# Spectral mixing and a feed-forward layer: a new start-up for the first batch, and a row operation that reads PSUM

## The chip, the cores and the metric

One core of one Trainium2 chip. The metric is the device time of one execution in microseconds (us). The kernel before took 1954.14 us (median of 3 runs, 1953.02 to 1954.99) when the prediction was made.

In what follows PE is the matmul engine, DVE the vector engine, ACT the scalar engine, POOL the general engine, and SP the engine that only issues DMAs. PSUM is the memory that PE writes to, cut into banks. "Half clock" means that the record of PE's granted clock shows 0.5.

## The reference

```python
batch, seq, dim = 8, 3008, 256
X = fft(fft(x, axis=1), axis=2).real           # Fourier mixing over sequence and features
h = X.reshape(24064, 256) @ w_in               # 256 -> 2048
g = h * (1 / (1 + exp(-1.702 * h)))            # quick GELU
out = g @ w_out                                # 2048 -> 256
```

## The kernel before

The sequence transform is done in two stages (3008 = 47 x 64). For each batch the rows of `x` are folded (even and odd parts), multiplied by cosine and sine tables, spilled to DRAM and read back in another order, rotated, and multiplied again ("stage 2"). Then 48 steps per batch form the hidden layer and the output: 384 steps in all, software-pipelined. "Nyquist's product" is a small extra product of one row, for the highest frequency; "warm-up" matmuls are products that nobody reads, there to keep PE busy and its clock up. A step makes two hidden products P and Q in two PSUM banks (`pa`, `pb`), builds two mirrored rows from their sum and difference, applies GELU, and feeds output products three steps later.

The parts that matter here are the start-up of the first batch and the rows of a step.

```python
def fold_first(r, m):                  # first batch, one of eight pieces
    ...
    nc.scalar.copy(dst(e[:], 0, H, 2), src(xt[:], 0, H, 2))                      # a tiny copy, on ACT
    nc.vector.tensor_tensor(dst(e[:], 1, 1, H - 1), ..., op=ALU.add)             # 128 partitions
    for p, eng in ((slice(0, 64), nc.vector), (slice(64, 128), nc.gpsimd)):      # DVE and POOL side by side
        eng.tensor_tensor(dst(e[p], H + 1, 1, H - 1), ..., op=ALU.subtract)

def mix_first(r, m):
    ...                                # matmuls of the piece into one bank
    nc.scalar.copy(xt[:, q:q + 2, :]..., ps[:])        # also ACT, in order with the tiny copy

def rows(t):
    ...
    nc.vector.tensor_tensor(two(h[:], n), two(v[:], n), two(pb[:], n), op=ALU.add)   # v: ACT's copy of pa
    ...                                # dif = nb * af2 - pb, twice
    ins = [... for x in (v, dif)]      # last row operation: two operands from SBUF
    nc.vector.tensor_tensor(free(h[:], 512 + at + m - 1, ...), *ins, op=ALU.add)

# start-up (cut)
for p in idle:                         # partitions of x's tile that hold no data are zeroed
    for eng, z in ((nc.vector, slice(0, 16)), (nc.gpsimd, slice(16, 32))):
        eng.memset(xt[p, z, :], 0.0)
load_in(0, nc.sync)                    # first weight chunk, ahead of x
nc.scalar.dma_start(out=w1[:], in_=tab1)
load_first(0, 4, nc.sync); load_first(4, 4, nc.scalar); load_first(8, 8, nc.sync)
...
for r in range(2):
    for m in range(4):
        fold_first(r, m)
        mix_first(r, m)
    spill(0, 8 * r, 8 * r + 8, (nc.sync, nc.scalar))
```

The weights arrive as 64-bit floats and are rounded on the core in eight chunks: three operations on ACT (`bounds`), three on DVE, and a clamp and an addition on POOL. In the kernel before, the first three chunks are given to `bounds` with `nc.gpsimd`: two of ACT's three operations are then on POOL. Rounding is spread over the start-up and the first steps.

## Time and profile before

| what | where it is read | before |
|---|---|---|
| PE busy over the whole run | busy shares | 98% |
| first hidden product starts | timeline | 63.91 us |
| seventh hidden product starts, PE dense from here | timeline | 104.54 us |
| PE busy from 148 to 1940 us | windows | 1792.00 of 1792.00 us |

The windows view of the kernel before shows how the start-up looked. Its columns are the stretch, its length, busy us of PE, of PE's weight load, of DVE, ACT and POOL, each with its count, then the granted clock, the DMA share and GB/s.

```profile
20.00:30.00 10.00, 4.61 (x18) 2.09 (x18) 10.00 (x8) 1.05 (x3) 9.55 (x6) 0.50 1.06 256
30.00:40.00 10.00, 5.94 (x26) 2.61 (x26) 10.00 (x10) 2.50 (x8) 7.66 (x6) 0.50 0.44 137
40.00:50.00 10.00, 8.08 (x28) 3.57 (x29) 0.92 (x1) 1.97 (x5) 3.47 (x2) 0.53 0.11 19
```

PE sits at half clock for almost all of it (last column but two). From 20 to 40 us DVE is busy all the time, and POOL nearly so; from 40 to 50 us they have finished their folds and PE still works through pieces that wait for each other on ACT.

### The profile page before, as it was taken

The numbers are of one execution on the slowest core, as the hardware profiler recorded it, in microseconds if no ns is written. First come the engines' busy times: TensorE is split into PE (matmuls) and PEld (weight loads), VectorE is DVE, ScalarE is ACT, GpSimd is POOL, SyncE is SP. The second block draws the span as 40 slices with busy tenths as digits, with TensorE's granted clock in tenths as the row PEclk, the third lists the DMA queues.
The fourth block names the chain that finished last, engine by engine and source line by source line (L and its number), as shares of the span: only waits on it lengthen the run. The fifth ranks groups of instructions, "written<-read, shape, count | busy, mean of one in ns | idle before, by whom it ended". The sixth has DMA issues, their size and how long they took to land.

```text
span 1952.1 us, 29356 instructions
## 1 busy us (share of the span) xinstructions
PE 1916.0 (98%) x10664; PEld 1672.3 (86%) x10664; DVE 1586.4 (81%) x2925; ACT 665.0 (34%) x921; POOL 816.1 (42%) x1057
## 2 busy tenths in 40 slices
PE   6899999999999999999999999999999999999998
PEld 2588888988889888898888888898888988889887
DVE  6688788888888887897788877888887888778876
ACT  1533333333333333333333333333333333333332
POOL 6476322652236432463225622265223643223222
PEclk6899999999999999999999999999999999999999
DMA  6732442227212282033621254322632224202201
GB/s 170 225 62 28 82 77 26 48 43 110 27 15 47 47 119 17 12 55 50 108 17 20 49 98 58 28 46 45 95 40 16 18 43 60 17 12 23 20 12 22
DMA packets 242311, 102.78 MB, mean 53 GB/s; under 512 B 207749, under 2 KB 232069, under 8 KB 238905
## 3 DMA queue, kind: packets, MB, share of 16 engines
q1 hardware_dynamic: 239154, 98.22, 32.5%
q10 hardware_dynamic: 3011, 2.69, 0.5%
q8 instruction: 83, 1.36, 0.3%
q14 instruction: 63, 0.51, 0.1%
HBM read 57.60 MB, written 47.67 MB: 54 GB/s over the span
## 4 chain that ended last, share of the span: by engine, by line
PE 96%; ACT 1%; DVE 0%; DVEq 0%; issue 0%
PE po L496 58%; PE pa L429 17%; PE pb L429 17%; PE ps L207 1%; PE ps L304 1%; PE psw L398 0%; PE ps L211 0%; PE psa L404 0%; ACT wcs L399 0%; ACT r L354 0%; ACT r L353 0%; ACT g L346 0%; PE psn L321 0%; ACT h L458 0%; ACT L458 0%; PE psr L291 0%
## 5 line engine op out<-in xcount | busy, mean ns | idle before, releaser
L470 POOL TENSOR_TENSOR s<-h 128x256 f32<-128x256 f32 (+1 forms) x376 | 269.5, 717 | 1060.5 <-ACT h L458 996.3
L496 PE MATMUL po<-s,wt 128*128 128x256 f32 (+1 forms) x2256 | 599.7, 375 | 0.0
L433 ACT COPY v<-pa 128x512 f32<-128x512 f32 (+1 forms) x384 | 221.8, 577 | 1065.0 <-PE pa L429 1064.9
L496 PEld LDWEIGHTS po<-s,wt 128*128 128x128 f32 x2256 | 428.6, 190 | 48.3
L443 DVE TENSOR_TENSOR h<-v,pb 128x512 f32<-128x512 f32 (+1 forms) x384 | 258.7, 674 | 260.0 <-PE pb L429 252.5
L496 PE MATMUL po<-h,wo 128*128 128x256 f32 (+1 forms) x1632 | 469.6, 375 | 0.0
L453 DVE TENSOR_TENSOR h<-v,dif 128x512 f32<-128x512 f32 (+1 forms) x448 | 413.4, 934 | 13.2
L458 ACT ACTIVATE h<-h 128x1024 f32<-128x1024 f32 (+1 forms) x384 | 400.7, 1043 | 19.6 <-DVE h L453 19.5
L429 PE MATMUL pa<-pq,wcs 128*128 128x256 f32 (+1 forms) x1536 | 395.8, 380 | 0.0
L429 PE MATMUL pb<-pq,wcs 128*128 128x256 f32 (+1 forms) x1536 | 388.8, 376 | 0.0
L496 PEld LDWEIGHTS po<-h,wo 128*128 128x128 f32 x1632 | 310.1, 190 | 35.5
L429 PEld LDWEIGHTS pa<-pq,wcs 128*128 128x128 f32 x1536 | 287.8, 191 | 47.8 <-issue 14.5
L446 DVE SCALAR_TENSOR_TENSOR dif<-nb,af,pb 128x256 f32<-128x256 f32 (+1 forms) x768 | 328.0, 468 | 0.5 <-DMA nb<-pq 0.5
L429 PEld LDWEIGHTS pb<-pq,wcs 128*128 128x128 f32 x1536 | 292.9, 191 | 33.6
L471 POOL TENSOR_TENSOR s<-h 128x256 f32<-128x256 f32 (+1 forms) x376 | 287.0, 763 | 0.0
L474 DVE TENSOR_TENSOR s<-h,s 128x256 f32<-128x256 f32 (+1 forms) x376 | 216.8, 576 | 13.0
L496 PE MATMUL po<-s,wo 128*128 128x256 f32 (+1 forms) x752 | 220.4, 375 | 0.0
L496 PE MATMUL po<-h,wt 128*128 128x256 f32 (+1 forms) x752 | 220.4, 375 | 0.0
L473 DVE TENSOR_TENSOR s<-s,h 128x256 f32<-128x256 f32 (+1 forms) x376 | 182.1, 484 | 4.7 <-POOL s L470 4.7
L496 PEld LDWEIGHTS po<-s,wo 128*128 128x128 f32 x752 | 142.9, 190 | 16.1
L496 PEld LDWEIGHTS po<-h,wt 128*128 128x128 f32 x752 | 142.9, 190 | 16.1
L193 POOL TENSOR_TENSOR xt<-xt 128x510 f32<-128x510 f32 x56 | 75.9, 1355 | 4.4
(66 smaller groups left out, 755.5 us busy)
## 6 DMA issues: line engine op xcount, KB each, us to landing
out_dram<-os SPq DMA_DIRECT2D x568, 32.0 KB
Td<-xt SPq DMA_DIRECT2D x14, 768.0 KB
t<-Td SPq DMA_DIRECT2D x7, 1536.0 KB
xt<-in_x_dram SPq DMA_DIRECT2D x15, 512.0 KB
nb<-pq SPq DMA_DIRECT2D x23, 256.0 KB
out_dram<-os SPq DMA_DIRECT2D x192, 28.0 KB
Xr<-in_x_dram SPq DMA_DIRECT2D x7, 752.0 KB
Xr<-in_x_dram SPq DMA_DIRECT2D x7, 705.0 KB
```

Of the source, the lines that this page charges most:

```text
L193: eng.tensor_tensor(low, low, free(t, up + D - 1, [-D, 2], [-1, D - 1]), op=ALU.add)
L429: nc.tensor.matmul(ps[:, i * 256:i * 256 + n], lhsT=wcs[cs][:, f * 128:(f + 1) * 128], rhs=pq[:, cs, ks], start=True, stop=True)
L433: nc.scalar.copy(two(v[:], n), two(pa[:], n))
L443: nc.vector.tensor_tensor(two(h[:], n), two(v[:], n), two(pb[:], n), op=ALU.add)
L446: nc.vector.scalar_tensor_tensor(dif[:, i * 256:i * 256 + n], nb[:, ks], af2[:, f:f + 1], pb[:, i * 256:i * 256 + n], op0=ALU.mult, op1=AL ...
L453: nc.vector.tensor_tensor(free(h[:], 512 + at + m - 1, [256, 2], [RUN, blocks], [-1, m]), *ins, op=ALU.add)
L458: nc.scalar.activation(g, g, ACTF.Gelu_apprx_sigmoid)
L470: eng.tensor_tensor(s1, a21, a22, op=ALU.add)
L471: eng.tensor_tensor(s3, a11, a21, op=ALU.subtract)
L473: eng.tensor_tensor(s2, s1, a11, op=ALU.subtract)
L474: eng.tensor_tensor(s4, a12, s2, op=ALU.subtract)
L496: nc.tensor.matmul(pot[q][:, i, :n], lhsT=lhs, rhs=rhs, start=(p == 0 and i == 0 and f == 0), stop=(p == NP - 1), skip_group_check=True)
```

## The change

Its intent is a shorter start-up. The first batch sits on 94 neighbouring partitions (2 x 47), so no partition of its tile has to be zeroed before loading and the fold needs no POOL; `x` is loaded ahead of the first weight chunk; each fold runs one piece ahead of its products; Nyquist's product moves behind the first hidden product; one weight chunk is rounded per step. `bounds` no longer gets `nc.gpsimd`, so two operations of each of the first three chunks move from POOL to ACT. Apart from that, the last row operation reads P's bank and not ACT's copy of it.

```diff
-    for p in idle:
-        for eng, z in ((nc.vector, slice(0, 16)), (nc.gpsimd, slice(16, 32))):
-            eng.memset(xt[p, z, :], 0.0)
-    load_in(0, nc.sync)
-    nc.scalar.dma_start(out=w1[:], in_=tab1)
+    nc.scalar.dma_start(out=w0, in_=tab1[:, 0:n0 + 1])
     load_first(0, 4, nc.sync)
     load_first(4, 4, nc.scalar)
     load_first(8, 8, nc.sync)
-    nc.sync.dma_start(out=small[:], in_=tab2)
+    nc.scalar.dma_start(out=small[:], in_=tab2)
+    load_in(0, nc.scalar)
...
+    fold_first(0)
+    for k in range(8):
+        if k < 7:
+            fold_first(k + 1)
+        else:
+            bounds(("in", 0))
+        mix_first(k)
+        if k % 4 == 3:
+            spill(0, 2 * k - 6, 2 * k + 2, (nc.sync, nc.scalar if k == 7 else nc.sync))
...
-                ins = [... for x in (v, dif)]
+                ins = [... for x in (pa, dif)]
...
         if t < n:
             hidden(t)
+        if t == 0:
+            nyquist_weights(0)
+            nyquist(0, 0)
```

Cut here: the tables (the first batch's sign is now folded into a second copy of the table, made by one DVE operation), the fold on 94 partitions with two DVE operations, the order of the rounding, loading the later batches' table during step 3, and the warm-up matmuls (`warm(10)` in place of `warm(12)` at the start, and a new `warm(4)` behind the last piece).

## The prediction

> **What bounds the kernel now.** I read the page's busy shares first, then the windows view (busy time of each engine by stretch), then the timeline of the first 110 us.
>
> ```profile
> PE 1916.0 (98%) x10664; PEld 1672.3 (86%) x10664; DVE 1586.4 (81%) x2925; ACT 665.0 (34%) x921; POOL 816.1 (42%) x1057
> ...
> 64.00:100.00 36.00, 33.99 (x132) 25.78 (x133) 28.90 (x34) 27.24 (x33) 15.22 (x9) 0.92 0.77 203
> 100.00:148.00 48.00, 47.32 (x298) 41.64 (x297) 38.44 (x64) 16.95 (x26) 33.86 (x40) 1.00 0.32 66
> 148.00:1940.00 1792.00, 1792.00 (x10046) 1584.05 (x10045) 1479.12 (x2789) 609.84 (x840) 727.81 (x984) 1.00 0.31 44
> 1940.00:1952.00 12.00, 3.88 (x18) 3.06 (x17) 3.89 (x9) 0.37 (x1) 0.00 (x0) 0.80 0.29 44
> ```
>
> In the last four lines the columns are the stretch, its length, then busy us of PE, PE's weight load, DVE, ACT and POOL, the clock, the DMA share and GB/s. From 148 to 1940 us PE is busy in 1792.00 of 1792.00 us at full clock. That matmul work is untouched by the change, so there is nothing to win there: only a new wait could lose something. Whatever is won lies before about 104 us, and shows as an earlier start of the dense part. So I follow the chain of the head.
>
> ```profile
> 14.48 1.28 ACT L346 ACT_TABLE_LOAD   x1 [14.48 <-DMA xt<-in_x_dram]
> 17.93 0.21 ACT L246 COPY e<-xt 128x8 f32<-128x8 f32 x1 [1.03 <-DMA xt<-in_x_dram]
> 39.20 0.58 ACT L262 COPY xt<-ps 128x512 f32<-128x512 f32 x1 [2.24 <-PE ps L259]
> 39.68 0.21 ACT L246 COPY e<-xt 128x8 f32<-128x8 f32 x1
> 39.99 1.98 PE L259 MATMUL ps<-e,w 128*64 128x256 f32 x8 [0.96 <-issue]
> 42.13 0.58 ACT L262 COPY xt<-ps 128x512 f32<-128x512 f32 x1 [2.24 <-PE ps L259]
> 48.62 0.37 ACTq L279 DMA_DIRECT2D Td<-xt  x1
> 53.60 0.38 SPq L285 DMA_DIRECT2D t<-Td  x1
> 57.81 0.56 PE L291 MATMUL psr<-t,small 128*128 128x4 f32 x2 [3.79 <-DMA t<-Td]
> 63.91 2.08 PE L429 MATMUL pa<-pq,wcs 128*128 128x256 f32 x4
> 83.52 0.69 DVE L453 TENSOR_TENSOR h<-v,dif 128x512 f32<-128x512 f32 x1
> 88.82 2.67 DVE L453 TENSOR_TENSOR h<-v,dif 128x512 f32<-128x512 f32 x1
> 104.54 1.13 PE L429 MATMUL pa<-pq,wcs 128*128 128x256 f32 x4
> ```
>
> These timeline lines give start, length, engine, operation and the idle time before. The first batch's folds start at 17.93, because the input arrives after a weight chunk, the tables and two memsets of its own tile. A piece then takes 2.93 us (39.20 to 42.13): matmuls 1.98 at half clock, their copy 0.58, then the tiny fold copy 0.21, on the same in-order engine behind it. The spill to DRAM is issued at 48.62; its result is back for the rotation at 57.81, the first hidden product is at 63.91, and the seventh, from which PE has no wait, at 104.54.
>
> **What the Trainium skill says.** "TensorE: Matmul & The Clock Gate", Part 1 on the clock gate: after an idle window of about 3.4 us PE falls to half clock, and needs about as long busy to come back. The trace agrees: the windows view has 1.00 from 0 to 10 us, 0.94 and 0.50 in the next two tens, with 7.1 us idle before the first fold product. "GPSIMD Engine Reference", Key points: it shares SBUF interfaces with VectorE and collides with instructions that have two SBUF inputs. It agrees: the fold sum takes 0.67 us, or 1.57 beside a busy POOL; the last row operation 0.69 or up to 2.67 (above). "DMA: Bandwidth & Descriptors", Queues, rings and completion order: each DMA engine takes packets in turn from the queues that have work. The DMA view of before agrees as far as it shows both queues moving at once (0.57 and 0.31 MB in the first five us).
>
> **The change, part by part.**
>
> *x first, and the memsets.* DMA is saturated from 2 to about 32 us. By bytes: in 10 to 25 us, mostly x, 0.89 + 0.95 + 0.81 MB took 15 us, so x runs at about 0.175 MB per us; wide rows (weight chunks, 25 to 30 us) reach 0.35 to 0.4. Before the last x piece lands the change still moves x (3.0 MB, 17.1 us), the table (0.82 MB, 2.1 us), and probably the small table and the first weight chunk (1.4 MB, 3.7 us), which sit on the other queue and take turns. With 1.9 us to start: about 25 us for the last piece, against some 26.5 before. The first piece lands at about 11 us instead of 17.9.
>
> *Folds ahead of products.* On 94 partitions POOL has no fold work left, so each fold is two DVE operations of 0.67 instead of up to 1.57 twice. Pieces 0 to 3 run in about 13 to 18 us. Then PE waits for x until about 25 (7 us idle), falls to half clock, and pieces 4 to 7 start at 25 + 1.4 = 26.5. The tiny copy is now ahead, so the pitch is PE's own 2.0 us instead of 2.93: the last ends at about 34.6. Here I see a price: ACT's three operations for the first weight chunk (1.12 + 1.06 + 1.06, about 3.3 us, the lengths of the trace) stand before the last copy out of PSUM. That copy starts about 36.5 and ends at 37.1, against 48.59 before.
>
> *Spill and return.* 48.6 to 57.8 is 9.2 us, mostly DMA round trips; the first half is spilled early but the return needs both. I keep 9.2: rotation at 46.3.
>
> *Rotation to hidden product.* Before 6.1 us. Nyquist (2.0 us) moves behind the first hidden product, and stage 2 (1.96 at half clock, 1.1 at full) may be faster: I take 3.5. First hidden product at about 49.8 instead of 63.9: minus 14.
>
> *The ramp.* Before it took 104.5 - 63.9 = 40.6 us to hidden product 7. Now it carries more: Nyquist and the first weight row (about 1.9 us on PE), and the rounding of out chunk 0. Per step DVE has about 2.3 us of rows and 1.23 + 0.69 + 1.23 of rounding, 5.4; ACT 3.3 of bounds, 0.58 + 1.06, and every second step 1.2 of weight copies, 4.9 to 6.1. PE itself has 1.7 hidden, 3.45 product from step 3, and 5.1 of weight folding every second step. All three are close, so little is absorbed. P's bank is now freed by the last row operation, not by ACT's copy; with four banks in turn, the weight row of the same step wants it. Measured in the trace of before, the end of that operation lies up to 3.9 us after the reuse of the bank in steps 0 to 5. Against that the operation reads PSUM, has one SBUF input and should cost 0.69 instead of 1.7 to 2.7 there. I take 42.5 us for the ramp: dense at 92.3, minus 12.
>
> *The steady part.* The last row operation drops from a mean of 1.06 to about 0.69 us, 320 x 0.37 = 120 us of DVE time. It is worth nothing: DVE isn't the bound. The bank is held longer; in the trace of before the smallest gap between the end of the last row operation and the reuse of P's bank is 0.57 us once the ramp is over (usually 4.7), except one step of the first batch (-1.0). Shorter operations widen that. I expect no wait.
>
> Sum: 1954.1 - 12 = 1942.
>
> **The rivals.** (1) x isn't overtaken by the small table and weight chunk, lands at 21 to 22, PE stays warm and the pieces finish four to six us sooner: 1936. For it: it is what the order is meant for; against it: turn-taking, and these two are issued at about 11 us, when half of x is outstanding. (2) The held bank makes PE wait in the ramp behind DVE, whose rounding is interleaved; each step loses one to two us: 1947 to 1950. For it: the negative gaps above; against it: the cheaper row operation. (3) The held bank stalls the dense part: even 0.3 us in each of 384 steps would be 115 us and 2060. Against it are the gaps of 0.57 and more, so I give it one in a hundred. (4) A large gain from freeing 120 us of DVE: excluded by PE's 1792.00.
>
> **Range and chances.** The terms that can move are x's arrival (+-3 us), the ACT detour (0 to 3) and the ramp (+-4). Together about +-7: 1935 to 1949. Faster by over 2% needs 39 us, more than the head has to give when dense must still start after 25 us of x and a 9 us round trip: 0.01.
>
> **What would show it.** Right: first fold copy at about 13, a PE gap of some 7 us ending near 26, clock 0.5 after it; the spill's second half issued near 37; rotation near 46; first hidden product near 50; PE's busy time equal to the stretch from about 95 on; last row operation near 0.69 us. Wrong: any PE wait on a DVE row operation after 150 us, a spill before 33 (rival 1), or a dense start after 97 (rival 2).

## The result

The changed kernel took 1941.72 us (median of 4 runs, 1941.08 to 1943.03), the kernel before 1954.07 us beside it (4 runs). The ratio is 0.9938, with a 95% interval from 0.9921 to 0.9955. A ratio here is the mean time of one kernel's runs over that of the other's of the same rounds, so it is not quite the ratio of the quoted medians. The predicted time was 1942.0.

The busy shares of the changed kernel:

```profile
PE 1908.7 (98%) x10730; PEld 1673.0 (86%) x10730; DVE 1409.5 (73%) x2924; ACT 671.6 (35%) x927; POOL 756.3 (39%) x1045
```

DVE has 1409.5 us of work in place of 1586.4, and PE is at 98% as it was. The windows view of the changed kernel, with columns as above:

```profile
20.00:30.00 10.00, 2.09 (x26) 1.88 (x24) 2.91 (x5) 1.20 (x4) 1.09 (x1) 0.80 1.07 244
30.00:40.00 10.00, 7.95 (x62) 5.51 (x58) 5.10 (x7) 7.38 (x11) 1.38 (x1) 0.86 0.49 160
40.00:50.00 10.00, 5.51 (x76) 2.93 (x77) 1.54 (x5) 5.18 (x8) 2.07 (x2) 0.99 0.71 237
...
136.00:1927.00 1791.00, 1791.00 (x10041) 1583.04 (x10040) 1323.47 (x2788) 609.94 (x839) 698.94 (x984) 1.00 0.31 44
```

The last line is the steady part: PE is again busy in every microsecond, 1791.00 of 1791.00. From 20 to 30 us, by contrast, nobody but the DMA has much to do (DMA share 1.07): everybody waits for `x`. The timeline of the changed kernel's start-up gives the chain:

```profile
13.85 5.01 DVE L251 TENSOR_TENSOR e<-xt 94x508 f32<-94x508 f32 x8 [5.89 <-DMA xt<-in_x_dram]
27.07 0.21 ACT L249 COPY e<-xt 94x8 f32<-94x8 f32 x1 [6.66 <-DMA xt<-in_x_dram]
28.52 5.80 PE L261 MATMUL ps<-e,wt 128*64 128x127 f32 x64 [7.91 <-DVE e L251]
34.01 1.14 ACT L346 ACTIVATE g<-raw 128x1024 f32<-128x1024 f32 x1
37.21 0.57 ACT L263 COPY xt<-ps 128x512 f32<-128x512 f32 x1
37.80 0.36 ACTq L279 DMA_DIRECT2D Td<-xt  x1
46.98 0.36 PE L291 MATMUL psr<-t,small 128*128 128x4 f32 x2 [2.24 <-DMA t<-Td]
49.63 1.85 PE L429 MATMUL pa<-pq,wcs 128*128 128x256 f32 x4 [1.21 <-DVE pq L310]
92.38 1.13 PE L429 MATMUL pa<-pq,wcs 128*128 128x256 f32 x4
```

Folds start at 13.85. `x`'s last piece lets ACT and DVE go on at 27.07, and PE's gap of 7.91 us ends at 28.52. Pieces 4 to 7 take 5.80 us of PE. Their last copy, however, starts at 37.21, because ACT does the first weight chunk from 34.01 on. The spill is issued at 37.80, the rotation starts at 46.98, the first hidden product at 49.63 and the seventh at 92.38. So the first hidden product comes 14.3 us earlier than before, and the seventh 12.2 us.

The waits of PE in the changed kernel up to 1940 us (what waited, for whom, us in total, times, longest) all lie in the start-up and the first steps. Lines shorter than 2 us are left out, except for one:

```profile
PE ps L261 <- DVE e L251: 7.9, 1, 7.9
PE psw L398 <- POOL wst L368: 3.1, 1, 3.1
PE ps L261 <- issue: 2.9, 1, 2.9
PE psr L291 <- DMA t<-Td: 2.2, 1, 2.2
PE psa L404 <- ACT wcs L399: 2.1, 3, 0.8
...
PE psw L398 <- DVE h L453: 1.4, 1, 1.4
```

The last one is where the held bank shows: PE's fold of a weight chunk wants a bank that the last row operation (L453) still reads, once. The 1.4 us are not its cost, though. The same fold also needs the weight chunk from POOL, and the timeline has both ending together:

```profile
68.47 2.37 POOL L368 TENSOR_TENSOR wst<-a,r 128x1024 uint32<-128x1024 uint32 x1
70.16 0.69 DVE L453 TENSOR_TENSOR h<-pa,dif 128x512 f32<-128x512 f32 x1
```

POOL's chunk is there at 70.84 and the bank is free at 70.85, so the bank alone cost PE 0.01 us at most.

The group of that row operation in the kernel before, with its busy us and mean ns:

```profile
L453 DVE TENSOR_TENSOR h<-v,dif 128x512 f32<-128x512 f32 x320 | 339.9, 1062 | 11.0
```

and in the changed kernel:

```profile
L453 DVE TENSOR_TENSOR h<-pa,dif 128x512 f32<-128x512 f32 x320 | 221.1, 691 | 11.0
```

From 1062 to 691 ns, 119 us of DVE in this form alone, and none of it is found in the steady part.

### The profile page after: what moved, and what is told of

The parts are those of the page before. It is cut to its first block, busy times and chain, and to the rows that moved or that the text cites. A ratio compares the mean times of both kernels' runs of the same rounds, so it can differ in the third digit from the quotient of the medians.

```text
span 1939.2 us, 29813 instructions
## 1 busy us (share of the span) xinstructions
PE 1908.7 (98%) x10730; PEld 1673.0 (86%) x10730; DVE 1409.5 (73%) x2924; ACT 671.6 (35%) x927; POOL 756.3 (39%) x1045
## 4 chain that ended last, share of the span: by engine, by line
PE 96%; DMA 2%; ACT 1%; DVE 0%; SPq 0%; issue 0%; DVEq 0%; ACTq 0%
PE po L496 59%; PE pa L429 17%; PE pb L429 17%; PE ps L211 1%; PE ps L304 1%; DMA xt<-in_x_dram 1%; DMA raw<-in_moe_w_in_dram 1%; PE psw L398 0%; PE ps L215 0%; DMA Td<-xt 0%; PE ps L261 0%; ACT g L346 0%; PE psa L404 0%; ACT wcs L399 0%; ACT r L353 0%
## 5 line engine op out<-in xcount | busy, mean ns | idle before, releaser
L470 POOL TENSOR_TENSOR s<-h 128x256 f32<-128x256 f32 (+1 forms) x376 | 270.3, 719 | 1093.4 <-ACT h L458 1028.5
L471 POOL TENSOR_TENSOR s<-h 128x256 f32<-128x256 f32 (+1 forms) x376 | 276.7, 736 | 0.0
L453 DVE TENSOR_TENSOR h<-pa,dif 128x512 f32<-128x512 f32 (+1 forms) x448 | 265.4, 604 | 13.2
L474 DVE TENSOR_TENSOR s<-h,s 128x256 f32<-128x256 f32 (+1 forms) x376 | 200.7, 534 | 12.9
L197 POOL TENSOR_TENSOR xt<-xt 111x510 f32<-111x510 f32 x56 | 74.1, 1323 | 4.4
```

The source lines that it names most:

```text
L197: eng.tensor_tensor(low, low, free(t, up + D - 1, [-D, 2], [-1, D - 1]), op=ALU.add)
L453: nc.vector.tensor_tensor(free(h[:], 512 + at + m - 1, [256, 2], [RUN, blocks], [-1, m]), *ins, op=ALU.add)
L470: eng.tensor_tensor(s1, a21, a22, op=ALU.add)
L471: eng.tensor_tensor(s3, a11, a21, op=ALU.subtract)
L474: eng.tensor_tensor(s4, a12, s2, op=ALU.subtract)
```

## The experiments

Twelve kernels were run in three sets of four, each in five rounds beside the kernel before on the same chip (`e3`, `e5`, `e9` and `e10` have four runs). The ratio to that kernel is what compares best between sets. The changed kernel itself was run again in the third set (`e11_after_again`).

| run | median us | ratio to before | 95% interval |
|---|---|---|---|
| `e11_after_again` (the changed kernel) | 1941.75 | 0.9939 | 0.9927 to 0.9952 |
| `e1_v_again` | 1942.89 | 0.9944 | 0.9931 to 0.9956 |
| `e2_row_only` (on the kernel before) | 1954.26 | 1.0005 | 0.9991 to 1.0019 |
| `e3_x_alone` | 1937.54 | 0.9919 | 0.9905 to 0.9932 |
| `e4_copy_first` | 1941.33 | 0.9940 | 0.9927 to 0.9952 |
| `e5_both_warm` | 1937.32 | 0.9917 | 0.9903 to 0.9930 |
| `e6_no_ahead` | 1942.29 | 0.9943 | 0.9929 to 0.9957 |
| `e7_weight_first` | 1943.34 | 0.9950 | 0.9938 to 0.9963 |
| `e8_nyquist_first` | 1942.75 | 0.9946 | 0.9934 to 0.9959 |
| `e9_warm_gap` | 1936.39 | 0.9914 | 0.9900 to 0.9927 |
| `e10_split_spill` | 1935.77 | 0.9910 | 0.9895 to 0.9925 |
| `e12_before_ahead` (on the kernel before) | 1949.91 | 0.9980 | 0.9968 to 0.9993 |

The intervals are some 2.5 us wide to either side, so differences of a microsecond between two rows are not settled by the times. Where I use one, I lean on the timelines too.

### The changed kernel again

No edit.

> The changed kernel unchanged, so that it stands beside the others on one chip: 1941 to 1943 us, ratio 0.993 to 0.995. If it shows 0.9945, the small losses of e1, e6 and e8 (0.9944, 0.9943, 0.9946) are none; at 0.9938 they are about 1 us each.

It came out at 0.9939, in another set, against 0.9938. So the small losses of the runs below are read as about one microsecond each, not as none, but inside their intervals.

Its trace shows how much one and the same kernel varies in the start-up:

```profile
28.32 6.54 PE L261 MATMUL ps<-e,wt 128*64 128x127 f32 x64 [8.20 <-DVE e L251]
```

Pieces 4 to 7 took 6.54 us here and 5.80 in the first profile, because the clock record came back to 1.00 at about 34.1 us and not at 32.8. The first hidden product started at 49.88 and the seventh at 92.06 (49.63 and 92.38 in the first). So events of two traces that lie some tenths apart are not told apart either.

### The row operation alone, both ways

```diff
# e1_v_again, on the changed kernel
-                ins = [... for x in (pa, dif)]
+                ins = [... for x in (v, dif)]
# e2_row_only, on the kernel before
-                ins = [... for x in (v, dif)]
+                ins = [... for x in (pa, dif)]
```

> The changed kernel, but the last row operation reads the copy v again and P's bank is freed by ACT's copy. Theory (the dense part is PE's, the row operation is worth nothing there, only some tenths in the ramp): 1940 to 1944 us against 1941.7; DVE busy back up by some 150 us; PE busy equal to the stretch from 136 to 1927 us as before. Rival A (freeing DVE is part of the gain): over 1945. Rival B (the held bank costs PE waits in the ramp): under 1940.

> The kernel before with nothing changed but the source of the last row operation (P's bank). Theory: 1951 to 1956 us, the same as before within 3 us, the mean of that operation at 128x512 near 0.69 us in place of 1.06. Rival A (freeing DVE is a good part of the gain): 1942 to 1949. Rival B (the held bank makes PE wait): over 1957.

Without the PSUM operand the changed kernel takes 1942.89 us, so the new start-up alone has nearly all of the gain (0.9944; 0.9939 with both). With it the kernel before takes 1954.26, beside 1953.59 in the same set, and its operation takes 691 ns as expected. The windows view of `e1_v_again`:

```profile
148.00:1924.00 1776.00, 1776.00 (x9967) 1568.82 (x9966) 1468.91 (x2768) 606.68 (x835) 712.95 (x972) 1.00 0.31 45
```

and of `e2_row_only`, the same stretch:

```profile
148.00:1924.00 1776.00, 1776.00 (x9973) 1569.90 (x9972) 1314.45 (x2773) 606.01 (x835) 694.32 (x978) 1.00 0.31 45
```

DVE's busy time differs by 154 us (1468.91 against 1314.45), PE's by nothing: 1776.00 of 1776.00 in both. In the same stretch the kernel before has 1468.90 of DVE and the changed kernel 1313.45, each again with 1776.00 of PE. This is the steady part settled: some 155 us less on an engine off the path, and a bank held longer, are both worth zero there. What is left of the row operation is in the first steps: from the first hidden product to the seventh `e1_v_again` takes 43.1 us, the changed kernel 42.8 and its rerun 42.2. That is 0.4 to 1.0 us, and 1.1 by the medians, which the intervals don't part from zero. Both rivals fall as they were stated: the time is neither over 1945 nor under 1940, and the kernel before stays at 1954, where they had 1942 to 1949 or over 1957.

### What delays x

```diff
# e3_x_alone
-    nc.scalar.dma_start(out=small[:], in_=tab2)
-    load_in(0, nc.scalar)
+    nc.sync.dma_start(out=small[:], in_=tab2)
+    load_in(0, nc.sync)
```

> The changed kernel with the small table and the first weight chunk behind x on the same queue, so that they can't take turns with x's last pieces. Theory (x's last piece is late because these 1.4 MB overtake it): it lands at 23 to 24 us in place of 27.0, PE's gap falls from 7.9 to 4 to 5 us, and all after it comes 3 to 3.5 us earlier: 1938 to 1939.5 us. Rival (the rate of x's narrow rows binds alone): x still at 26 to 27 us, 1941 to 1942.5.

The mechanism was right, and the gain somewhat larger than the theory's range: 1937.54 us, 4.2 us less than the changed kernel. The timeline of `e3_x_alone`:

```profile
23.26 5.79 DVE L251 TENSOR_TENSOR e<-xt 94x508 f32<-94x508 f32 x8 [4.19 <-DMA xt<-in_x_dram]
24.68 5.62 PE L261 MATMUL ps<-e,wt 128*64 128x127 f32 x64 [3.78 <-DVE e L251]
...
33.77 0.37 ACTq L279 DMA_DIRECT2D Td<-xt  x1
```

`x` is there at 23.26 in place of 27.07, PE's gap is 3.78 in place of 7.91, and the spill is issued 4.0 us earlier. The DMA view of the changed kernel from 15 to 20 us (queue, packets, MB, share) shows the same thing from the other side. Queue 10 is ACT's, with the small table and the weight chunk; queue 1 is SP's, with `x`:

```profile
q10 hardware_dynamic: 426, 1.43, 88.6%
q1 hardware_dynamic: 220, 0.22, 15.2%
```

Both had transfers issued, and ACT's queue got 1.43 MB while `x` got 0.22. By this view a packet of ACT's queue carried 3.4 KB and one of `x` 1.0 KB on average, so even with equal turns `x` would have got the smaller part. "x loaded first" was undone by the second queue.

```diff
# e7_weight_first
+    load_in(0, nc.sync)
     nc.scalar.dma_start(out=w0, in_=tab1[:, 0:n0 + 1])
...
-    load_in(0, nc.scalar)
```

> The changed kernel with the first weight chunk loaded ahead of x, as in the kernel before (the memsets of x's tile stay gone). Theory (the chunk overtakes x's last pieces anyway, so the same bytes stand before the last piece): first fold 2 to 3 us later, at 16 to 17; last piece at 26 to 28 as with x first; 1941 to 1943 us. Rival (x first is a part of the gain, and the last piece comes 2.7 us later, the chunk's time on the DMA): 1944 to 1945.5.

My theory failed here. The last piece came at 30.06 in the timeline, 3.0 us later than with `x` first, which is what the rival had said of it, and the median was 1943.34, between theory and rival (1944 to 1945.5). So loading `x` ahead of the chunk is worth something, about 1.6 us of the 12.4 by the medians. The small table still stood on ACT's queue, and the timeline doesn't tell which of these bytes cost the last piece how much.

### The copy behind the weight chunk, and the clock

```diff
# e4_copy_first
-        if k < 7:
-            fold_first(k + 1)
-        else:
-            bounds(("in", 0))
+        if k < 7:
+            fold_first(k + 1)
         mix_first(k)
...
+    bounds(("in", 0))
```

> The changed kernel with ACT's three operations for the first weight chunk behind the last copy out of PSUM, not before it. Theory (they hold that copy, and the spill, 2.9 us): the copy starts at about 34.3 in place of 37.2, the spilled data is back at about 44; but the folding of the first weight chunk stands before the rotation on PE and starts some 0.6 us later than 41.0 and takes 3.7, so the rotation starts at about 45.3 in place of 47.0: 1939.5 to 1940.5 us. Rival (the weight chunk is as critical as the spill): 1941.5 to 1942.5.

The first half was right, the second not. The timeline of `e4_copy_first`:

```profile
33.99 0.59 ACT L263 COPY xt<-ps 128x512 f32<-128x512 f32 x1 [0.29 <-PE ps L261]
34.60 0.37 ACTq L279 DMA_DIRECT2D Td<-xt  x1
...
42.03 5.38 PE L398 MATMUL psw<-wst,small 128*128 128x512 f32 x8 [4.49 <-POOL wst L368]
47.26 0.28 PE L291 MATMUL psr<-t,small 128*128 128x4 f32 x2
```

The spill is issued 3.2 us earlier. But the weight chunk is ready only at 42.03, PE has idled 4.49 us by then, and its fold takes 5.38 us in place of 3.70, partly at half clock. The rotation, which comes behind it in PE's program, starts at 47.26, no earlier than 46.98. 1941.33 us is near the rival's range, and the reason is that a second chain of equal length (weight chunk, fold) lay beside the spill. The slow fold is not the edit's alone: in the rerun of the changed kernel it took 5.21 us as well, from 41.31, and the rotation started at 47.23.

```diff
# e5_both_warm: e3 and e4 together, and
-    warm(4)
+    warm(8)
# e9_warm_gap: e5, and in the loop over pieces
+        if k == 3:
+            warm(4)
# e10_split_spill: e9, and the second spill as pieces 4 to 6, then 7
```

> The changed kernel with both: x alone on its queue and the last copy first, and eight warm-up matmuls in place of four behind the last piece, so that PE doesn't fall to half clock before it folds the first weight chunk (in e4 that cost 1.7 us and the whole gain). Theory: x lands at 23.3, the spill is issued at about 30.3 and is back at 39.5; the weight chunk is ready at 37.6 and is folded by 41.3 at full clock; rotation at 41.3, first hidden product at 44 in place of 46.3 in e3: 1935 to 1936 us against 1937.5 of e3. Rival (the weight chunk, not the spill, sets the start in e3): 1937 to 1938.

A miss: 1937.32 us, the rival's range, no better than `e3_x_alone`. In its timeline the pieces 4 to 7 ran at half clock:

```profile
25.59 6.55 PE L261 MATMUL ps<-e,wt 128*64 128x127 f32 x64 [5.42 <-DVE e L251]
...
32.83 0.37 ACTq L279 DMA_DIRECT2D Td<-xt  x1
```

The spill was expected at about 30.3. Of the 2.5 us that it was late, 0.8 are `x`, which landed at 24.1 in this run and not at 23.3; the rest was put down to the clock. The rival was right about `e3_x_alone` as well: there PE folds the weight chunk from 37.03 for 6.56 us, mostly at half clock, and the rotation follows at 43.42 without a wait. Here the fold starts at 40.27, as the chunk now comes behind the last copy, and the rotation at 43.81. The reading of the clock was tested by keeping PE busy in the gap.

> e5 with four warm-up matmuls in the wait for x after piece 3. Theory (in e5 PE fell to half clock in that wait, so pieces 4 to 7 took 6.6 us and the spill was issued at 32.8): the pieces follow DVE's folds at 1.4 us each, the spill is issued at about 31, the weight chunk is folded from 38, first hidden product at 44 to 45 in place of 46.6: 1935 to 1936.5 us against 1937.3. Rival (the folds and the DMA set that stage, not the clock): 1937 to 1938.

1936.39 us, inside the theory's range, though the intervals don't part it from `e5_both_warm`. The windows view from 20 to 40 us has the clock at 1.00 (in e5 0.73 and 0.93), and the timeline of `e9_warm_gap` shows the chain that is left:

```profile
31.60 0.37 ACTq L279 DMA_DIRECT2D Td<-xt  x1
...
39.03 3.70 PE L398 MATMUL psw<-wst,small 128*128 128x512 f32 x8 [1.08 <-POOL wst L368]
42.57 0.28 PE L291 MATMUL psr<-t,small 128*128 128x4 f32 x2
```

The spill is 1.2 us sooner than in e5, the weight fold starts 1.2 us sooner, and the rotation follows the fold without a wait. The first hidden product is at 45.40, 1.2 us sooner than in e5 and a little later than the 44 to 45 of the theory. The weight chunk still sets the start.

> e9 with the second spill in two parts, three pieces and then one, so that the last transfer is a quarter of it. Theory (the round trip is partly transfer: 0.77 MB in some 2.5 us): data back about 1 us sooner, but PE folds the weight chunk until about 42 anyhow, so at most 1 us: 1934.5 to 1936.5 us, equal to e9 or up to 1 us less. Rival (the first part queues in front of the second and costs): 1 us more than e9.

1935.77 us, in the theory's range and 0.6 below e9, which the intervals don't separate. Its trace gives the split no credit: the rotation starts at 42.38 and not 42.57, and `x` had landed 0.16 us sooner. Both runs beat the changed kernel of the same set by more than 5 us (0.9910 and 0.9914 against 0.9939), and each of their runs is shorter than the shortest of its runs (1937.43 at most against 1940.58 at least).

### Folds ahead, taken out and put in

```diff
# e6_no_ahead
-    fold_first(0)
     for k in range(8):
-        if k < 7:
-            fold_first(k + 1)
-        else:
+        fold_first(k)
+        if k == 7:
             bounds(("in", 0))
# e12_before_ahead: the kernel before, with
+    fold_first(0, 0)
...
-            fold_first(r, m)
+            if (r, m) != (1, 3):
+                fold_first(*divmod(4 * r + m + 1, 4))
             mix_first(r, m)
```

> The changed kernel with each fold directly before its own products, so that ACT's small fold copy stands behind the copy of the piece before, as in the kernel before. Theory: pieces 0 to 3 hide in the wait for x; pieces 4 to 7 go at 2.9 us each at half clock (2.0 if the clock is full) in place of 1.4, and the spill is issued 1 to 3.5 us later than 37.8: 1942.5 to 1945 us. Rival (everything in this stage hides behind x and the DMA): 1941 to 1942.

The runs fell between the two: 1942.09, 1942.19, 1942.29, 1943.93 and 1945.35 us. The profile is of the slowest. There the spill is issued at 41.02, 3.2 us later than 37.80, with a clock of 0.55 from 30 to 40 us. But 1.3 of the 3.2 are not the edit's: `x`'s last piece landed at 28.39 in this run and at 27.07 in the other. The copies of pieces 4 to 6 start at 31.90, 34.28 and 36.66, so a piece takes 2.38 us at half clock, not the 2.9 of the theory, against 1.70 in the changed kernel. The faster runs have no trace. Their mean granted clock is higher (0.995 for the three of 1942, 0.993 and 0.992 for the others), so a clock that changes at another moment would fit, but that, and when `x` landed in them, is not shown.

> The kernel before with nothing changed but each fold one piece ahead of the products (its folds stay on 128 partitions, DVE and POOL side by side). Theory: pieces no longer wait for the copy behind them, but DVE's two folds of 1.57 beside POOL (3.1 us a piece) become the pitch; DVE's last fold ended at 40.9, so the last copy ends at about 43.5 to 44 in place of 48.6: 1948.5 to 1950.5 us. Rival (running ahead is worth nothing without taking POOL out): 1953 to 1955.

On the kernel before the same idea alone gives 3.3 us: 1949.91. Its timeline:

```profile
36.69 1.58 DVE L250 TENSOR_TENSOR e<-xt 64x508 f32<-64x508 f32 x1
38.20 1.51 DVE L247 TENSOR_TENSOR e<-xt 128x508 f32<-128x508 f32 x1
39.63 0.67 DVE L250 TENSOR_TENSOR e<-xt 64x508 f32<-64x508 f32 x1
...
43.21 0.38 ACTq L279 DMA_DIRECT2D Td<-xt  x1
```

The spill goes out 5.4 us earlier than the 48.62 of before (1.4 of it were there at the first fold already, 18.69 against 20.14, and are not the edit's). What holds it now are DVE's folds, two for each piece and about 1.5 us each beside a busy POOL. At 36.69 and 38.20 POOL no longer folds: its timeline has the rounding of the next weight chunk there (L350 from 36.30, L351 from 37.82 to 40.91). The last fold takes 0.67, though L351 still runs; why is not shown. The change takes both kinds of work off POOL in this stage, and the changed kernel's eight folds of pieces 4 to 7 take 4.87 us together, 0.61 each.

### Nyquist in its old place

```diff
# e8_nyquist_first
+    nyquist_weights(0)
     rotate(0, 0, 4, nc.scalar.copy)
     stage2(0, 0)
+    nyquist(0, 0)
...
-        if t == 0:
-            nyquist_weights(0)
-            nyquist(0, 0)
```

> The changed kernel with Nyquist's product and the first weight row ahead of the first hidden product, as before. Theory (in the ramp PE has waits that take the 2 us up): first hidden product about 2 us later than 49.6, but the second and later ones at most 1 us later: 1941.5 to 1943 us. Rival (all of it is on the path): 1943.5 to 1944.5.

1942.75 us, in the theory's range, which reaches down to the changed kernel's own time. In its trace the first hidden product starts at 52.30, 2.7 us later than 49.63, and the seventh at 93.78 against 92.38, 1.4 later where the theory had at most 1 (2.4 and 1.7 against the rerun). So by these traces a third to a half of the move was taken up by waits that the first steps have anyway.

## Why the prediction was right

The time was 1942.0 predicted and 1941.72 measured, and most of the chain holds term by term; two terms were off by some 2 us, in opposite directions. The first fold copy was late too, 1.3 us of it behind ACT's table load at 13.62, but that cost nothing, since PE waited for the last piece of `x` anyway. The "ramp" is the stretch from the first hidden product to the seventh.

| step of the prediction | predicted | measured |
|---|---|---|
| first fold copy | about 13 | 14.91 |
| last piece of x lands | about 25 | 27.07 |
| pieces 4 to 7 end on PE | 34.6 | 34.3 (28.52 + 5.80) |
| last copy out of PSUM ends | 37.1 | 37.78 (37.21 + 0.57) |
| rotation starts | 46.3 | 46.98 |
| rotation to first hidden product | 3.5 | 2.65 |
| first hidden product | 49.8 | 49.63 |
| ramp to the seventh | 42.5 | 42.75 |
| dense from | 92.3 | 92.38 |

**x.** The step "small table and weight chunk take turns with x" was right, and `e3_x_alone` shows it. Its sum came out 2 us too small. Turn-taking isn't the part that was mis-sized, for the sum had put all bytes of the other queue ahead of `x`'s end (1.9 + 17.1 + 2.1 + 3.7 = 24.8). The rate of `x` is a part: from 20 to 25 us, with SP's queue nearly alone, the DMA view has 0.83 MB, 0.166 MB per us in place of 0.175, an estimated 1 us over 3.0 MB. The rest is not located.

**The pieces.** I took 2.0 us for each, at half clock to the end, from 26.5. They started at 28.5 and took 5.80 us in all. A part is the clock: the record has 0.50 from 26.0 to 32.8 us, so it came back before the last piece. The larger part is the size of a piece: at half clock the copies of pieces 4 and 5 start 1.70 us apart (30.58 and 32.28), not 2.0; the 1.98 was read where each piece began after a pause. In the rerun, at half clock almost to the end, the four took 6.54 us. The term "PE's own 2.0 us" was mis-sized by 2 us in all, and this hid the late `x`. It is luck that the two cancel.

**The detour on ACT** was seen in advance and is there: three operations from 34.01, and the last copy 2.9 us after PE had finished. What the prediction did not see is that removing it brings nothing by itself: `e4_copy_first` shows a second chain, the first weight chunk, which ends as late.

**Spill and return** was kept at 9.2 and measured at 9.18 (37.80 to 46.98).

**Ramp and bank.** The 1.4 us wait put down to the last row operation is the one that rival 2 named, but POOL's weight chunk ended it just as late (70.84 against 70.85), so the held bank cost next to nothing. The ramp stayed within 0.3 us of the estimate. In `e1_v_again`, where the bank is free early and the operation dear, the first hidden product is at 49.34 and the seventh at 92.48, a ramp that is 0.4 us longer (1.0 against the rerun). Rival 2 is excluded with it.

**The steady part.** No wait appeared; freeing 154 us of DVE gave nothing, and e1 and e2 show it from both sides. Rivals 3 and 4 are excluded. Rival 1 (x not overtaken) described a better kernel than the changed one: forced in `e3_x_alone`, `x` landed at 23.3 and not 21 to 22, and the time was 1937.54 where 1936 had been said.

**A reading.** The prediction took a clock of 1.00 from 0 to 10 us as agreeing with the Trainium skill. That record is doubtful: in the same trace the weight loads of the warm-up matmuls are 0.85 us apart until 5.03 us and 0.43 from 5.50 on, so PE seems to have begun at half clock there too. Nothing in the sum rests on it.

How the 12.4 us split over the parts is known only in part. One by one, 1.6 us go with the order of `x` and the chunk (e7), 1.0 with Nyquist (e8), 1.1 with the row operation (e1), all by medians whose intervals overlap with the changed kernel's, and 0.5 by the median with running ahead (e6; up to 3.6 in the slowest run, where `x` was late); on the old kernel running ahead gives 3.3 (e12). They may interact, as some can hide behind `x`, and need not add up. The memsets and the 94 partitions could not be put back alone without rewriting tables and folds, so their share stays open, and so does that of the rounding which left POOL.

## What to carry to other kernels

When one engine is busy in every microsecond of the steady part, only the start-up and the end are left. There, follow the chain from event to event and look for the second-longest chain beside it, because shortening one alone may give nothing. Loading something "first" did not hold across two DMA queues here: a large transfer on the other queue delayed it, and with that transfer behind it on the same queue it landed at 23.26 and not 27.07. And an idle gap of PE can cost twice, once as a gap (7.91 us) and once as half clock after it (until 32.8).

## What the Trainium skill lacked or had wrong

- "DMA: Bandwidth & Descriptors", section Queues, rings and completion order, says that an engine takes packets in turn from its queues. It doesn't say how unequal the bytes can be: from 15 to 20 us the changed kernel's ACT queue got 1.43 MB and the SP queue 0.22 MB, both with transfers issued. In packets it was 426 to 220, so the size of a packet (3.4 against 1.0 KB) makes the larger part of it; why the packets stand two to one is not shown.
- "TensorE: Matmul & The Clock Gate", Part 1, gives a busy window of some 3.4 us for the return to full clock, but not how much idle time such a window may hold. Before, PE was busy in about 1.98 of every 2.93 us from 37.06 to 47.8 us and the clock stayed at 0.50. In `e6_no_ahead` it was busy in 1.97 of every 2.38 us from 32.64 to 37.4 us, and the clock stayed at 0.50 to 39 us.
- "VectorE: DVE Perf Modes", in its section on the TRN2 errata, lists a higher fixed cost for a PSUM source than for an SBUF source. For the last row operation no difference shows: 691 ns on average with one operand in PSUM, 0.69 us with both in SBUF with POOL not at work beside it (`e1_v_again` at 56.48). The section doesn't say what holds when only one of two sources is in PSUM.
